# Three of seven local-attention value products on GpSimd, the activation's sign moved into w_in's columns

## The chip, the core and the metric

One core of a Trainium2 chip runs the whole program. The metric is device time in microseconds (us), the median of the runs of one program. The engines have an instruction queue each and run it strictly in order: PE (TensorE, matrix products; PEld is its weight load), DVE (VectorE), ACT (ScalarE), POOL (GpSimd) and SP, which here only issues the DMA transfers. An instruction whose input is not there yet holds up everything behind it on its engine. POOL works on on-chip SBUF only; the results of PE stand in PSUM, which DVE and ACT can read and write.

## The reference, cut to what matters

```python
B, H, S, D, factor = 8, 8, 576, 64, 4
# attention, per batch and head
q_d, k_d, v_d = means over 4 neighbouring tokens                # 144 tokens
out_up    = repeat(softmax(q_d @ k_d.T / 8) @ v_d, 4)
out_local = softmax(where(|i - j| < 4, q @ k.T / 8, -1e9)) @ v  # 7 neighbours of each token
x = (out_up + out_local) as 4608 tokens x 512
# feed-forward
h = x @ w_in                                                    # 512 -> 2048
g = maximum(h, 0) + alpha * minimum(h, 0)                       # alpha per column
out = g @ w_out                                                 # 2048 -> 512
```

The inputs of the feed-forward arrive as 64-bit floats and are decoded on the chip.

## The kernel before, in words

The work has three strands that share the engines.

**Weights** (`load_weights`, L159). w_in and w_out come in four parts n = 0 to 3 of 512 columns or rows. A piece of 128x512 lands as raw 64-bit words; `decode` (L150) turns it into `temp` with one ACT and four DVE instructions (L152 to L156). Then it is split into a high and a low half of reduced precision: ACT writes the high one (`wih`, L206, `woh`, L203), and the low one is the difference (`wil` on DVE, L210, or on POOL through `sub`, L97; `wol` on DVE, L204). For w_out each row is multiplied on the way by `sign`, which is +1 where alpha is at most 1 and -1 elsewhere. The raw pieces take turns in a few slots, and SP can issue the next only when a slot is free. Part 3 goes through other buffers, once the first batch's attention is done.

**Feed-forward.** Tokens go in 18 chunks of 256, columns in 8 pairs of 128, so there are 144 steps. `h_step` (L633) has 24 matmuls (L642) into `ph`, then the activation: ACT writes t = slope*h for each of the two columns (L651), DVE takes the maximum of sign*h and t for each of the two (L654, `sign` as a scalar of each partition), ACT writes the high half `gh` (L656), POOL the low half `gl` = t - gh (L97). `out_step` (L680) has 12 matmuls (L690) with gh and gl. The h step stands two steps ahead of its out step (AH = 2).

**Attention.** The first batch is done ahead on PE. From batch 1 on, `local` (L532) takes units of 192 tokens, u = 3 to 23, on DVE: a token's row lies on a partition as two heads x 6 tokens, its keys and values with three neighbours on either side. It does the score products and sums for two halves of three tokens (L551, L553), the softmax, and the value products: for each half the acc of neighbour 0 (L593), products of neighbours 1 to 3 and of 4 and 5 (L596), five additions to acc (L598). Neighbour 6 is multiplied on POOL (L580), one instruction for each half, and the last DVE addition joins it (`x`, L600). acc and the weights of the neighbours stand in the PSUM tile `lb`. PE transposes x (L607), and `xf`, `xh` and `xl` become the feed-forward's operands. Beside it `down` (L237) does the attention over the means: for each pair of heads SP loads six tiles (`ldq`, `ldk`, `ldv`, two each, L228) into three buffers, POOL adds neighbours in them (L231) and writes the sums (`s2q`, `s2k`, `s2v`, L232), which gives the buffer back; PE transposes the sums (L249) and so on. There is one s2q and one s2k, so the next is written when PE has transposed the last.

**What sets the order.** The code interleaves the generators of units, downs and steps; a scheduler then fixes each engine's list, with priorities (`high_priority`) for the activation. k and q of a unit have one buffer each, v has two, and a unit's loads are issued by SP in line with the ld loads. An ld tile that lands late holds up POOL, and with it every gl behind it.

Of the kernel before, what the change touches and what calls it, by code (L numbers as in the profile page):

```python
# [9 lines left out]
F32 = mybir.dt.float32  # L10
# [3 lines left out]
ALU = mybir.AluOpType  # L14
# [32 lines left out]
LDB = 3  # L47
SB = 2
# [21 lines left out]
def tile_attention_moe(ctx: ExitStack, tc: tile.TileContext, q, k, v, w_in, w_out, alpha, out):  # L70
# [22 lines left out]
    def f32(ap):  # L93
        return ap.bitcast(F32)
# [39 lines left out]

    def load_alpha():
        nc.sync.dma_start(slope, alpha.rearrange("(f p) -> p f", p=128))
        nc.vector.tensor_scalar(sign, slope, 1.0, 2.0, op0=ALU.is_le, op1=ALU.mult)
        nc.vector.tensor_scalar(sign, sign, -1.0, None, op0=ALU.add)
        nc.vector.tensor_tensor(slope, slope, sign, op=ALU.mult)
# [19 lines left out]
    def load_weights():  # L159
        temp, turn = one.tile([128, 4, 512], I32, tag="slot3", name="temp"), 0  # L160
        for n in range(4):
            if n in (1, 2):
                for i, x in enumerate("hl"):
                    wi[i][n] = one.tile([128, 4, 512], F32R, tag=f"spare{8 - 4 * n + i}", name=f"wi{x}{n}")
                    wo[i][n] = one.tile([128, 4, 512], F32R, tag=f"spare{10 - 4 * n + i}", name=f"wo{x}{n}")
            for which, w in enumerate((wi, wo)):
# [5 lines left out]
                for c0 in (0, 2):  # L172
# [17 lines left out]
                    for r, c, m in pieces:  # L190
# [341 lines left out]
    def local(late, u):  # L532
# [27 lines left out]
        if jj != 1:  # L560
# [13 lines left out]
        nc.vector.tensor_tensor(ex[:, :, 6], ex[:, :, 6], rs, op=ALU.mult)  # L574
        nc.vector.tensor_tensor(pw[:, :, 0:6], ex[:, :, 0:6],
                                rs.unsqueeze(2).to_broadcast([128, 2, 6, 6]), op=ALU.mult)
        pv6 = []
        for half in range(2):
            t = late.tile([128, 2, 3, 64], F32, tag="pp", name=f"pv6_{u}_{half}", bufs=2)
            nc.gpsimd.tensor_tensor(  # L580
                t, window4(vt, half, 6, 1)[:, 0],
                ex[:, half, 6].rearrange("p (h t) -> p h t", h=2).unsqueeze(3).to_broadcast([128, 2, 3, 64]),
                op=ALU.mult)
            pv6.append(t)
        yield
        x = late.tile([128, 6, 2, 64], F32, tag="x", name=f"x{u}", bufs=XB)
# [5 lines left out]
        for half in range(2):  # L592
            nc.vector.tensor_tensor(acc, window4(vt, half, 0, 1)[:, 0], prob(half, 0, 1)[:, 0], op=ALU.mult)  # L593
            for d0, nd in ((1, 3), (4, 2)):
                pr = late.tile([128, 3, 2, 3, 64], F32, tag="prod", bufs=PB, name=f"pv{u}_{half}{d0}")
                nc.vector.tensor_tensor(pr[:, :nd], window4(vt, half, d0, nd), prob(half, d0, nd), op=ALU.mult)  # L596
                for i in range(nd):
                    nc.vector.tensor_tensor(acc, acc, pr[:, i], op=ALU.add)  # L598
                yield
            nc.vector.tensor_tensor(x[:, 3 * half:3 * half + 3].rearrange("p t h d -> p h t d"),  # L600
                                    acc, pv6[half], op=ALU.add)
# [31 lines left out]
    def h_step(st):  # L633
# [14 lines left out]
        with tc.high_priority(offset=HP):  # L648
# [3 lines left out]
            for j in range(2):  # L652
                f = 2 * fp + j
                nc.vector.scalar_tensor_tensor(t[:, j], ph[:, j], sign[:, f:f + 1], t[:, j],  # L654
                                               op0=ALU.mult, op1=ALU.max)
# [185 lines left out]
```

## Time and profile before

| what | value |
|---|---|
| median of 3 runs | 1140.39 us (1134.49, 1140.88, 1140.39) |
| profiled execution | 1138.52 us |
| its span, first to last instruction | 1136.7 us |
| mean granted TensorE clock | 0.926 |

In the rows of the prediction, a group reads: line, engine, operation, result <- inputs (by the program's names), shape, xcount | busy us, mean ns of one | idle time of the engine just before, and what ended it. A row of waits reads: engine, line <- what was waited for: us in total, times, longest. A row of a stretch reads: from:to, length, then the busy time of each engine and, in brackets, the number of its instructions. A row of the chain of work that ended last reads: start us, length us, what.

### The profile page before, as it was taken

The numbers are of one execution on the slowest core, as the hardware profiler recorded it, in microseconds if no ns is written. First come the engines' busy times: TensorE is split into PE (matmuls) and PEld (weight loads), VectorE is DVE, ScalarE is ACT, GpSimd is POOL, SyncE is SP. The second block draws the span as 40 slices with busy tenths as digits, with TensorE's granted clock in tenths as the row PEclk, the third lists the DMA queues.
The fourth block names the chain that finished last, engine by engine and source line by source line (L and its number), as shares of the span: only waits on it lengthen the run. The fifth ranks groups of instructions, "written<-read, shape, count | busy, mean of one in ns | idle before, by whom it ended". The sixth has DMA issues, their size and how long they took to land.

```text
span 1136.7 us, 17891 instructions
## 1 busy us (share of the span) xinstructions
PE 1005.7 (88%) x6402; PEld 879.8 (77%) x6402; DVE 861.4 (76%) x1467; ACT 454.7 (40%) x1223; POOL 526.4 (46%) x633
## 2 busy tenths in 40 slices
PE   5857797898768999889999999989999989999995
PEld 5646675696657898777888888878888878899994
DVE  7999496597847889678878988779887778895110
ACT  5767344242323443333444334344343425333221
POOL 4787474333434644544555543555537244333221
PEclk9756889798968999899999999999999989999998
DMA  8944612222222222221223222323222212100000
GB/s 181 240 150 145 189 43 86 65 83 76 66 92 77 87 100 87 92 87 65 80 95 109 85 80 89 105 76 101 88 92 82 96 58 78 54 19 19 1 20 19
DMA packets 57503, 98.26 MB, mean 86 GB/s; under 512 B 19910, under 2 KB 25286, under 8 KB 57414
## 3 DMA queue, kind: packets, MB, share of 16 engines
q1 hardware_dynamic: 57414, 97.12, 27.1%
q8 instruction: 50, 0.82, 0.3%
q14 instruction: 39, 0.32, 0.1%
HBM read 87.67 MB, written 9.44 MB: 85 GB/s over the span
## 4 chain that ended last, share of the span: by engine, by line
PE 53%; DMA 20%; DVE 11%; POOL 6%; SPq 4%; issue 3%; ACT 2%; ACTq 0%; POOLq 0%; DVEq 0%
PE o L690 26%; PE h L642 22%; DMA ldk<-in_k 10%; DMA q<-in_q 4%; DMA ldq<-in_q 3%; POOL gl L97 2%; SPq L348 2%; DVE temp L155 1%; SPq L499 1%; POOL ldv L100 1%; DVE temp L153 1%; PE pv L266 1%; DVE temp L156 1%; PE xp L607 1%; DMA raw<-in_moe_w_out 1%
## 5 line engine op out<-in xcount | busy, mean ns | idle before, releaser
L97 POOL TENSOR_TENSOR gl<-t,gh 128x512 fp32r<-128x512 f32 x144 | 187.0, 1301 | 238.5 <-ACT gh L656 221.3
L654 DVE SCALAR_TENSOR_TENSOR t<-h,sign,t 128x256 f32<-128x256 f32 x288 | 125.6, 478 | 165.1 <-ACT t L651 159.3
L690 PE MATMUL o<-woh,gl 128*128 128x512 f32 x576 | 193.7, 414 | 45.1 <-POOL gl L97 45.0
L651 ACT ACTIVATE t<-h,slope 128x256 f32<-128x256 f32 x288 | 120.3, 469 | 244.4 <-PE h L642 159.4
L642 PE MATMUL h<-xh,wih 128*128 128x256 f32 x1152 | 201.1, 291 | 1.0 <-DVE t L654 0.7
L690 PE MATMUL o<-woh,gh 128*128 128x512 f32 x576 | 190.2, 407 | 10.3 <-ACT gh L656 10.3
L642 PE MATMUL h<-xh,wil 128*128 128x256 f32 x1152 | 194.3, 288 | 1.0 <-DVE wil L210 1.0
L690 PE MATMUL o<-wol,gh 128*128 128x512 f32 x576 | 191.2, 409 | 0.0
L642 PE MATMUL h<-xl,wih 128*128 128x256 f32 x1152 | 188.0, 285 | 0.0
L642 PEld LDWEIGHTS h<-xh,wih 128*128 128x128 f32 x1152 | 174.0, 196 | 14.4 <-DVE t L654 2.4
L690 PEld LDWEIGHTS o<-woh,gl 128*128 128x128 f32 x576 | 110.4, 195 | 75.8 <-POOL gl L97 51.7
L642 PEld LDWEIGHTS h<-xh,wil 128*128 128x128 f32 x1152 | 163.1, 194 | 1.9 <-DVE wil L210 1.2
L642 PEld LDWEIGHTS h<-xl,wih 128*128 128x128 f32 x1152 | 159.9, 192 | 0.3
L656 ACT CAST gh<-t 128x512 fp32r<-128x512 f32 x144 | 89.4, 621 | 148.5 <-PE o L690 78.6
L551 DVE TENSOR_TENSOR qk<-k,qp 128x768 f32<-128x768 f32 (+1 forms) x126 | 135.0, 1081 | 0.0
L553 DVE TENSOR_REDUCE ls<-qk 128x12 f32<-128x768 f32 (+1 forms) x126 | 133.5, 1080 | 0.2
L690 PEld LDWEIGHTS o<-wol,gh 128*128 128x128 f32 x576 | 111.1, 195 | 24.9 <-issue 0.2
L690 PEld LDWEIGHTS o<-woh,gh 128*128 128x128 f32 x576 | 102.3, 194 | 25.2 <-ACT gh L656 10.5
L598 DVE TENSOR_TENSOR lb<-lb,pv 128x384 f32<-128x384 f32 x210 | 117.9, 562 | 4.0
L100 POOL TENSOR_TENSOR ldk<-ldk 72x256 f32<-72x256 f32 x56 | 45.2, 808 | 153.7 <-DMA ldk<-in_k 143.3
L596 DVE TENSOR_TENSOR pv<-v,lb 128x1152 f32<-128x1152 f32 x84 | 96.8, 1152 | 2.5
L100 POOL TENSOR_TENSOR ldq<-ldq 72x256 f32<-72x256 f32 x56 | 42.8, 774 | 80.6 <-DMA ldq<-in_q 80.4
(146 smaller groups left out, 1194.3 us busy)
## 6 DMA issues: line engine op xcount, KB each, us to landing
k<-in_k SPq DMA_DIRECT2D x41, 384.0 KB
v<-in_v SPq DMA_DIRECT2D x41, 384.0 KB
raw<-in_moe_w_in SPq DMA_DIRECT2D x16, 512.0 KB
raw<-in_moe_w_out SPq DMA_DIRECT2D x16, 512.0 KB
ldq<-in_q SPq DMA_DIRECT2D x56, 144.0 KB
ldk<-in_k SPq DMA_DIRECT2D x56, 144.0 KB
ldv<-in_v SPq DMA_DIRECT2D x56, 144.0 KB
q<-in_q SPq DMA_DIRECT2D x42, 192.0 KB
```

Source lines behind the costliest of these rows:

```text
L97: nc.gpsimd.tensor_tensor(o, a, b, op=ALU.subtract)
L100: nc.gpsimd.tensor_tensor(o, a, b, op=ALU.add)
L348: nc.sync.dma_start(qk[hp][:, i, :, e, :], bass.AP(src.tensor, (2 * hp + e) * HEAD, [[512, 72], [64, 8], [1, 64]]))
L551: nc.vector.tensor_tensor(pr[:, :nd], window(kt, half, d0, nd), qp.unsqueeze(1).to_broadcast([128, nd, 2, 192]), op=ALU.mult)
L553: nc.vector.tensor_reduce(out=s[:, half, d0:d0 + nd, :].rearrange("p a b -> p (a b)"), in_=pr[:, :nd].rearrange("p a h (t d) -> p (a h t) ...
L596: nc.vector.tensor_tensor(pr[:, :nd], window4(vt, half, d0, nd), prob(half, d0, nd), op=ALU.mult)
L598: nc.vector.tensor_tensor(acc, acc, pr[:, i], op=ALU.add)
L642: nc.tensor.matmul(ph[:, j], w[:, m, 128 * o:128 * o + 128], x[:, m, :], start=(i == 0), stop=(i == 11))
L651: nc.scalar.activation(t[:, j], ph[:, j], AF.Copy, scale=slope[:, f:f + 1])
L654: nc.vector.scalar_tensor_tensor(t[:, j], ph[:, j], sign[:, f:f + 1], t[:, j], op0=ALU.mult, op1=ALU.max)
L656: nc.scalar.copy(gh, t)
L690: nc.tensor.matmul(po, g[:, j, 128 * m:128 * m + 128], wo[w][n][:, o, :], start=(f == 0 and i == 0), stop=(f == NF - 1 and i == 2))
```

## The change

1. Of the seven neighbours, 4, 5 and 6 (`FAR` = 3) now go to POOL: for each half three products and two additions there, the first product straight into x's tile. DVE keeps neighbours 0 to 3 (one product of one, one of three, three additions) and adds acc to what POOL left in x. v is read by POOL three times as often, and its buffer is free when both engines are done.
2. The sign leaves the activation: w_in's columns are multiplied by it (a DVE instruction for each of w_in's 16 pieces of 128x512, before the halves are taken), from a row of signs that is made once for each n from a DMA of alpha to all partitions and two DVE instructions. The rows of w_out keep theirs. ACT's slope is now alpha itself.
3. The two maxima of a step become one, of 128x512, of ph and t.

```diff
+FAR = 3
+    def to_sign(o, a):
+        nc.vector.tensor_scalar(o, a, 1.0, 2.0, op0=ALU.is_le, op1=ALU.mult)
+        nc.vector.tensor_scalar(o, o, -1.0, None, op0=ALU.add)
...
-        nc.vector.tensor_tensor(slope, slope, sign, op=ALU.mult)
+        to_sign(sign, slope)
+    def column_signs(n):
+        row = two.tile([128, DM], F32, tag="stage", name=f"srow{n}", bufs=SB)
+        nc.sync.dma_start(row, bass.AP(alpha.tensor, 512 * n, [[0, 128], [1, 512]]))
+        to_sign(row, row)
+        return row
...
+            srow = column_signs(n)
...
                             else:
+                                nc.vector.tensor_tensor(f32(t), f32(t), srow.unsqueeze(1).to_broadcast([128, m, 512]), op=ALU.mult)
                                 nc.scalar.copy(wh, f32(t))
...
+        ND = 7 - FAR
+        x = late.tile([128, 6, 2, 64], F32, tag="x", name=f"x{u}", bufs=XB)
+        xs = [x[:, 3 * half:3 * half + 3].rearrange("p t h d -> p h t d") for half in range(2)]
         for half in range(2):
-            t = late.tile([128, 2, 3, 64], F32, tag="pp", name=f"pv6_{u}_{half}", bufs=2)
-            nc.gpsimd.tensor_tensor(
-                t, window4(vt, half, 6, 1)[:, 0],
...
+            for i, dl in enumerate(range(ND, 7)):
+                o = xs[half] if i == 0 else late.tile([128, 2, 3, 64], F32, tag="pp", name=f"pv{dl}_{u}_{half}", bufs=2)
+                nc.gpsimd.tensor_tensor(
+                    o, window4(vt, half, dl, 1)[:, 0],
...
+                if i:
+                    add(xs[half], xs[half], o)
+            yield
...
         for half in range(2):
             nc.vector.tensor_tensor(acc, window4(vt, half, 0, 1)[:, 0], prob(half, 0, 1)[:, 0], op=ALU.mult)
-            for d0, nd in ((1, 3), (4, 2)):
-                pr = late.tile([128, 3, 2, 3, 64], F32, tag="prod", bufs=PB, name=f"pv{u}_{half}{d0}")
-                nc.vector.tensor_tensor(pr[:, :nd], window4(vt, half, d0, nd), prob(half, d0, nd), op=ALU.mult)
-                for i in range(nd):
-                    nc.vector.tensor_tensor(acc, acc, pr[:, i], op=ALU.add)
-                yield
-            nc.vector.tensor_tensor(x[:, 3 * half:3 * half + 3].rearrange("p t h d -> p h t d"),
-                                    acc, pv6[half], op=ALU.add)
+            pr = late.tile([128, 3, 2, 3, 64], F32, tag="prod", bufs=PB, name=f"pv{u}_{half}")
+            nc.vector.tensor_tensor(pr, window4(vt, half, 1, 3), prob(half, 1, 3), op=ALU.mult)
+            for i in range(3):
+                nc.vector.tensor_tensor(acc, acc, pr[:, i], op=ALU.add)
+            yield
+            nc.vector.tensor_tensor(xs[half], acc, xs[half], op=ALU.add)
...
-            for j in range(2):
-                f = 2 * fp + j
-                nc.vector.scalar_tensor_tensor(t[:, j], ph[:, j], sign[:, f:f + 1], t[:, j],
-                                               op0=ALU.mult, op1=ALU.max)
+            nc.vector.tensor_tensor(t, ph, t, op=ALU.max)
```

The scheduler also gives every engine another order. Three places follow; before's lines are those of the kernel before, the others those of the changed kernel (L595 and L101 are the products and additions on POOL, L614 is the last addition on DVE, L665 the maximum, L203 the raw loads, L239 the ld loads).

POOL around unit 8, before: the products of neighbour 6 and what stands behind them up to the next two gl.

```order
L97 TENSOR_TENSOR gl_4201<-t_4199,gh_4200 128x512
L580 TENSOR_TENSOR pv_8_0_3826<-v_3170,lex_3767 128x384
L580 TENSOR_TENSOR pv_8_1_3828<-v_3170,lex_3767 128x384
L100 TENSOR_TENSOR ldv_20_4083<-ldv_20_4083 72x2x128
L100 TENSOR_TENSOR ldv_21_4087<-ldv_21_4087 72x2x128
L100 TENSOR_TENSOR ldq_30_4263<-ldq_30_4263 72x2x128
L100 TENSOR_TENSOR s2v_2_4082<-ldv_20_4083 72x2x64
L100 TENSOR_TENSOR s2v_2_4082<-ldv_21_4087 72x2x64
L97 TENSOR_TENSOR gl_4298<-t_4296,gh_4297 128x512
```

POOL at the same place now, from the first product of unit 8 to the first addition of its second half.

```order
L595 TENSOR_TENSOR pv_8_0_3794<-v_3185,lex_3731 128x384
L595 TENSOR_TENSOR x_3789<-v_3185,lex_3731 128x2x3x64
L98 TENSOR_TENSOR gl_4155<-t_4153,gh_4154 128x512
L101 TENSOR_TENSOR ldq_30_4272<-ldq_30_4272 72x2x128
L101 TENSOR_TENSOR x_3789<-x_3789,pv_8_0_3791 128x2x3x64
L98 TENSOR_TENSOR gl_4239<-t_4237,gh_4238 128x512
L101 TENSOR_TENSOR ldq_31_4276<-ldq_31_4276 72x2x128
L101 TENSOR_TENSOR ldk_30_4288<-ldk_30_4288 72x2x128
L101 TENSOR_TENSOR x_3789<-x_3789,pv_8_0_3794 128x2x3x64
L595 TENSOR_TENSOR pv_8_1_3807<-v_3185,lex_3731 128x384
L98 TENSOR_TENSOR gl_4343<-t_4341,gh_4342 128x512
L101 TENSOR_TENSOR x_3789<-x_3789,pv_8_1_3807 128x2x3x64
```

Ten instructions of the unit are spread over the ld adds and the gl, where two stood in a row; ld adds that wait for a transfer now stand between a half's products and its last addition.

DVE in unit 8, before: from the end of the first half to the second half's first products (t is the maximum of a step).

```order
L654 SCALAR_TENSOR_TENSOR t_4296<-h_4271,sign,t_4296 128x256 x2
L598 TENSOR_TENSOR lb_3766<-lb_3766,pv_01_3841 128x384
L596 TENSOR_TENSOR pv_04_3846<-v_3170,lb_3766 128x768
L598 TENSOR_TENSOR lb_3766<-lb_3766,pv_04_3846 128x384 x2
L600 TENSOR_TENSOR x_3839<-lb_3766,pv_8_0_3826 128x2x3x64
L593 TENSOR_TENSOR lb_3766<-v_3170,lb_3766 128x384
```

DVE at the same place now.

```order
L612 TENSOR_TENSOR lb_3730<-lb_3730,pv_0_3814 128x384 x2
L665 TENSOR_TENSOR t_4237<-h_4212,t_4237 128x512
L665 TENSOR_TENSOR t_4341<-h_4316,t_4341 128x512
L614 TENSOR_TENSOR x_3789<-lb_3730,x_3789 128x2x3x64
L608 TENSOR_TENSOR lb_3730<-v_3185,lb_3730 128x384
```

The addition that joins POOL's part now stands two maxima later, and the second half, which uses the same acc, stands behind it.

SP near the end of the start, before: the pieces of w_in's part 3 (raw_1036, raw_1055) among the loads.

```order
L228 DMA ldk_20_1402<-in_k 72x512
L193 DMA raw_1036<-in_moe_w_in 128x1024 x2
L228 DMA ldk_21_1406<-in_k 72x512
L193 DMA raw_1055<-in_moe_w_in 128x1024 x2
L228 DMA ldv_20_1411<-in_v 72x512
```

SP now (raw_1063 and raw_1084 are those pieces).

```order
L239 DMA ldq_31_1560<-in_q 72x512
L239 DMA ldk_30_1565<-in_k 72x512
L203 DMA raw_1063<-in_moe_w_in 128x1024 x2
L239 DMA ldk_31_1569<-in_k 72x512
L239 DMA ldv_30_1574<-in_v 72x512
L203 DMA raw_1084<-in_moe_w_in 128x1024 x2
```

The last part of w_in is loaded one down later than before; in exchange the ld loads of the downs behind it stand ahead of the next v and q.

More of the change, by code (lines that the diff above doesn't have):

```diff
@@ L573, in local @@
         acc = lb[:, 0:384].rearrange("p (h t d) -> p h t d", h=2, t=3)
[L574 to L577, printed above, removed]
-        for half in range(2):
-            t = late.tile([128, 2, 3, 64], F32, tag="pp", name=f"pv6_{u}_{half}", bufs=2)
-            nc.gpsimd.tensor_tensor(
-                t, window4(vt, half, 6, 1)[:, 0],
-                ex[:, half, 6].rearrange("p (h t) -> p h t", h=2).unsqueeze(3).to_broadcast([128, 2, 3, 64]),
-                op=ALU.mult)
-            pv6.append(t)
-        yield
-        x = late.tile([128, 6, 2, 64], F32, tag="x", name=f"x{u}", bufs=XB)
+        ND = 7 - FAR
+        nc.vector.tensor_tensor(ex[:, :, ND:], ex[:, :, ND:], rs.unsqueeze(2).to_broadcast([128, 2, FAR, 6]), op=ALU.mult)
+        nc.vector.tensor_tensor(pw[:, :, 0:ND], ex[:, :, 0:ND],
+                                rs.unsqueeze(2).to_broadcast([128, 2, ND, 6]), op=ALU.mult)
+        x = late.tile([128, 6, 2, 64], F32, tag="x", name=f"x{u}", bufs=XB)
+        xs = [x[:, 3 * half:3 * half + 3].rearrange("p t h d -> p h t d") for half in range(2)]
+        for half in range(2):
+            for i, dl in enumerate(range(ND, 7)):
+                o = xs[half] if i == 0 else late.tile([128, 2, 3, 64], F32, tag="pp", name=f"pv{dl}_{u}_{half}", bufs=2)
+                nc.gpsimd.tensor_tensor(
+                    o, window4(vt, half, dl, 1)[:, 0],
+                    ex[:, half, dl].rearrange("p (h t) -> p h t", h=2).unsqueeze(3).to_broadcast([128, 2, 3, 64]),
+                    op=ALU.mult)
+                if i:
+                    add(xs[half], xs[half], o)
+            yield
         def prob(half, d0, nd):
```

3 lines of the change are left out of this document (removed).

## The prediction

> **What bounds the kernel now.** I read first how busy each engine is over the whole span, then the chain of work that ended last, then stretches of time, and last the waits of the stretch that turned out to matter. The page's own lines:
>
> ```profile
> span 1136.7 us, 17891 instructions
> PE 1005.7 (88%) x6402; PEld 879.8 (77%) x6402; DVE 861.4 (76%) x1467; ACT 454.7 (40%) x1223; POOL 526.4 (46%) x633
> ...
> PE 53%; DMA 20%; DVE 11%; POOL 6%; SPq 4%; issue 3%; ACT 2%; ACTq 0%; POOLq 0%; DVEq 0%
> ```
>
> PE is the bound on average, but of the chain it holds only 53%, and transfers hold 20%: there are places where PE waits. The stretches tell them apart. A row gives from:to, length, busy time of PE, PEld, DVE, ACT and POOL with instruction counts, then the granted clock, the DMA share and GB/s.
>
> ```profile
> 0.00:50.00 50.00, 34.02 (x212) 29.73 (x213) 41.31 (x79) 30.48 (x79) 26.20 (x43) 0.90 0.93 199
> 50.00:100.00 50.00, 32.31 (x222) 25.82 (x221) 48.85 (x81) 32.91 (x95) 40.09 (x34) 0.53 0.51 160
> 213.00:960.00 747.00, 689.51 (x4433) 605.42 (x4434) 611.90 (x1038) 290.89 (x808) 354.11 (x457) 0.96 0.25 84
> 360.00:460.00 100.00, 99.97 (x671) 89.27 (x670) 92.29 (x158) 43.81 (x119) 45.61 (x56) 1.00 0.27 93
> 960.00:1137.00 177.00, 164.50 (x1050) 147.35 (x1048) 82.75 (x153) 52.74 (x117) 45.36 (x39) 0.98 0.07 24
> ```
>
> The start (0 to 213) decodes weights; 213 to 960 is the steady part, where units, downs and steps run together; behind it only steps are left. From 0 to 50 the DMA engines are the full ones (0.93), from 50 to 100 DVE is (48.85 of 50). How far the steady part is from its own best pace is seen by counting the two feed-forward lines in it and in its best 100 us. First the h matmuls (L642), then the out matmuls (L690); the columns are PE and PEld of that line alone:
>
> ```profile
> 213.00:960.00 747.00, 337.39 (x2508) 322.03 (x2508) 0.96 0.25 84
> 360.00:460.00 100.00, 50.96 (x388) 48.66 (x388) 1.00 0.27 93
> ```
>
> ```profile
> 213.00:960.00 747.00, 336.75 (x1256) 233.86 (x1256) 0.96 0.25 84
> 360.00:460.00 100.00, 49.34 (x193) 34.66 (x192) 1.00 0.27 93
> ```
>
> A step has 24 + 12 = 36 of them. The steady part does (2508 + 1256) / 36 = 104.6 steps at 7.14 us, the best stretch (388 + 193) / 36 = 16.1 steps at 6.20. So the steady part loses 104.6 x 0.94 = 98 us against a pace that this kernel itself reaches, with PE at 99.97 and DVE at 92.29 of 100. DVE's load does not set the pace there, then; something stops PE now and then. The waits of that stretch (what waits <- for what: us, times, longest):
>
> ```profile
> POOL ldk L100 <- DMA ldk<-in_k: 128.7, 23, 16.9
> POOL gl L97 <- ACT gh L656: 107.5, 31, 9.2
> POOL ldq L100 <- DMA ldq<-in_q: 59.7, 23, 10.2
> PE o L690 <- POOL gl L97: 45.0, 16, 5.7
> DVE x L600 <- POOL pv L580: 13.5, 6, 6.0
> SPq L520 <- DVE pv L596: 92.0, 12, 23.2
> ```
>
> PE's largest wait is for gl on POOL, 45.0 us; POOL in turn stands 128.7 + 59.7 = 188.4 us before ld tiles that have not landed. The chain shows one such ring (start, length, what):
>
> ```profile
> 284.68 0.14 PE qkT L249 x2
> ...
> 284.88 0.47 POOL s2q L100
> 285.37 10.38 DMA ldk<-in_k
> ```
>
> PE's transposes free s2q, POOL writes the next sums, that frees an ld buffer, SP loads into it for 10.38 us, and POOL waits at the next ld add, with gl behind it and PE behind gl. Of every us that POOL waits for ld transfers, 45.0 / 188.4 = 0.24 reaches PE; I use 0.24 as the price of a late POOL or SP.
>
> **The change part by part.** The instructions concerned, as groups (busy us, mean ns of one | idle before it):
>
> ```profile
> L654 DVE SCALAR_TENSOR_TENSOR t<-h,sign,t 128x256 f32<-128x256 f32 x288 | 125.6, 478 | 165.1 <-ACT t L651 159.3 <-POOL gl L97 1.7 <-POOL s2v L100 1.4
> L598 DVE TENSOR_TENSOR lb<-lb,pv 128x384 f32<-128x384 f32 x210 | 117.9, 562 | 4.0
> L596 DVE TENSOR_TENSOR pv<-v,lb 128x768 f32<-128x768 f32 x42 | 40.0, 952 | 1.2
> L580 POOL TENSOR_TENSOR pv<-v,lex 128x384 f32<-128x384 f32 x42 | 34.0, 828 | 3.8 <-PE o L690 3.3 <-issue 0.3
> ```
>
> *DVE is relieved.* Per half the product of neighbours 4 and 5 and two additions go: 42 x (0.952 + 2 x 0.562) = 87.2 us. 288 maxima of 256 become 144 of 512. None of that size is in the trace; the DVE rows of 384 (0.562) and 768 (0.952) bound one, and a third of the way between them is 0.692, so 99.6 us stand for 125.6, 26 less (between 45 less and 11 more). Together 113 us, of which some 100 fall in the steady part. All of it would count if DVE set the pace, but the best stretch says that it doesn't. What a freer DVE does is to give buffers back earlier: SP waits 12 times for DVE's products, 92.0 us, with ld loads queued behind. Each product chain of a unit is 4.2 us shorter (2 x 2.08), so those waits shrink by at most 12 x 4.2 = 50 us; times 0.24 that is 12 us. I take **-12**, with 0 (the ring of the transposes has no DVE in it) and -49 (half of the 98) as ends.
>
> *POOL is loaded, and tied to DVE.* 84 products more at 0.828 are 69.6 us. 84 additions of 384 lie between these rows of the steady part, which also show the load adds:
>
> ```profile
> L97 POOL TENSOR_TENSOR gl<-t,gh 128x512 fp32r<-128x512 f32 x106 | 136.0, 1286 | 120.1 <-ACT gh L656 107.5 <-PE o L690 7.1 <-PE h L642 4.3
> ...
> L100 POOL TENSOR_TENSOR ldk<-ldk 72x256 f32<-72x256 f32 x45 | 33.0, 734 | 138.5 <-DMA ldk<-in_k 128.7 <-DVE pv L596 9.8
> L100 POOL TENSOR_TENSOR ldq<-ldq 72x256 f32<-72x256 f32 x44 | 31.7, 731 | 60.0 <-DMA ldq<-in_q 59.7 <-PE pT L293 0.3
> ```
>
> Halfway between 734 and 1286 is 1.01 us, so 84.7 us: 154 us in all, 7.3 per unit. In the steady part POOL now has 354.1 busy and 188.4 waiting for ld tiles, 542.5 of 747 (73%); with 19 units of 7.3 it has 681 (91%) if the waits stay. So POOL does not become the bound, but its slack goes from 27% to 9%. The Trainium skill (GPSIMD Engine Reference, section Performance versus the Vector engine) says that an elementwise operation of two inputs takes GpSimd about twice DVE's time. The rows here give 828 against 562 for 384 elements, 1.47 times. By the page the moved work would be an estimated 168 x 2 x 0.562 = 189 us instead of 154, and the sum some 8 us higher; the row is of this very shape, and I stay with it.
>
> The larger part is the order. Before, two POOL products stand in a row early in the unit, and DVE waited for them only 13.5 us. Now ten POOL instructions stand spread, and in 18 of 21 units adds of ldq or ldk stand between the first product and the last addition, 47 of them in all. About half of such adds wait (23 of 45 and 23 of 44), 188.4 / 46 = 4.1 us each: 23.5 x 4.1 = 96 us that DVE's final addition of a half can now wait for. What is queued behind that on DVE is the second half (same acc), and the maxima of the following steps, hence gh, gl and PE's out step. At 0.24 that is **+23**. Lower end 0: DVE's spare 100 us absorb it. Upper end 48, half of it. By another reading, the moved instructions that stand between an ld add and the next gl (47 against 14) delay gl by 0.7 us net at each of 16 stalls, +11; both fall on the same waits, so only the larger counts. v is now given back by the slower of two engines; that too is a part of this term.
>
> *The start.* 16 column products of 128x512 and 8 instructions that make the sign rows are new on DVE. Rows of the start (groups, then single instructions with the wait before them in brackets):
>
> ```profile
> L156 DVE SCALAR_TENSOR_TENSOR temp<-raw,temp 128x512 int32<-128x512 int32 x32 | 27.5, 864 | 0.1
> L153 DVE TENSOR_SCALAR temp<-temp 128x512 f32<-128x512 f32 x32 | 22.6, 709 | 11.3 <-ACT temp L152 11.3
> ...
> L210 DVE TENSOR_TENSOR wil<-temp,wih 128x512 fp32r<-128x512 f32 x11 | 10.9, 995 | 0.0
> ```
>
> ```profile
> 135.49 1.96 DVE L153 TENSOR_SCALAR temp<-temp 128x512 f32<-128x512 f32 x1 [8.13 <-ACT temp L152]
> ...
> 142.68 3.02 DVE L156 SCALAR_TENSOR_TENSOR temp<-raw,temp 128x512 int32<-128x512 int32 x1
> ```
>
> 16 x 0.995 + 8 x 0.709 = 21.6 us, 5.4 for each of four parts. The first lies in 0 to 50, where DVE is idle 8.7 us behind the transfers: nothing. The second and third fall in 50 to 100, where DVE is full: 10.8 on the path. The fourth comes behind 135, with the loads of part 3. The DVE wait of 8.13 at 135.49 takes up half of these 16.2; I take **+8**. Upper end 32: the products stretch to 3.02 each, as that one row did beside POOL work, (3.02 - 0.995) x 16. Lower end -14, from SP's order: the ld loads stand ahead of v and q now, and POOL's longest wait for one between 181 and 213 could go. Against it, w_in's part 3 is issued one down later. That wait:
>
> ```profile
> POOL ldk L100 <- DMA ldk<-in_k: 13.9, 1, 13.9
> ```
>
> The sign rows' four DMAs are 256 KB each on the chip's side, beside 512 KB pieces from 0 to 50; hidden there.
>
> *The rest.* The slopes and signs per column are tiny. ACT and PE keep their counts. Behind 960 DVE has 82.75 of 177, and the merged maximum is hidden by that idle time.
>
> Sum: 8 - 12 + 23 = +19 on the profiled execution's 1138.52 (span and 1.8 around it): 1157.5. That execution is 1.9 under the median of 1140.39, so **1159**.
>
> **The rivals.** *The relief reaches PE (faster).* If the rings close faster because SP's loads for DVE-held buffers no longer delay the ld loads, and POOL's additions fit into its waits, half of the 98 us comes back and the coupling costs nothing: 1138.5 + 8 - 49 + 1.9 = 1099. For it speak the 92.0 us of SP's waits for DVE products and the 125.6 us of maxima on the path from ph to gl, which DVE does sooner; against it the ring above, in which DVE has no part. It decides where DVE's final additions wait for POOL under some 40 us in all.
>
> *It cancels (same).* If the ld adds between the moved instructions are seldom late, only the +11 counts: 1138.5 + 8 - 12 + 11 + 1.9 = 1147. For it speaks that half of the adds didn't wait before.
>
> *DVE and POOL block each other (slower still).* The row at 142.68 took 3.02 us where 32 of its kind took 0.864 on average, and POOL was at work there. If each column product waits so, the start costs +32 more than the work, and 8 + 32 - 12 + 23 gives 1138.5 + 51 + 1.9 = 1191. The Trainium skill (SBUF — State Buffer, section Who interferes with whom) has such a rule: a DVE instruction with two SBUF inputs and a GpSimd instruction that reads SBUF exclude each other, the second waits for the whole of the first. Against it stands the mean of L210, 995 ns, with two SBUF inputs and POOL busy up to 40.09 of 50: most are not held up for long.
>
> *The change doesn't do what it says:* DVE's relief is eaten by waits for POOL. That is the mechanism of my forecast.
>
> **How the numbers follow.** Against the median, 1% is 1129.0 and 1151.8, about what a measurement of this kernel can tell from no change. The forecast has 0.48 and its own range of 1152 to 1182 (the coupling from +16 to +46); blocking 0.06, beyond 1182; cancelling 0.16; the relief 0.30. So slower 0.54, same 0.16, faster 0.30. The range has to hold both signs: its low end is the relief's own 1098, below which half of that case's 0.30 lies, its high end 1195, just past the blocking rival's 1191, with 0.05 beyond. That leaves out 0.2.
>
> **What would show it.** In the changed profile, from 213 to 960: DVE's wait for POOL at the last addition grows from 13.5 to some 100 us; POOL's busy share rises from 47% to about 66%; PE's wait for gl rises from 45.0 towards 70; DVE's busy time falls by some 100. In the start, 50 to 100 stays full on DVE, the first steady out step comes some 8 us later, and the column products take about 1.0 us (0.7 to 1.0). The forecast is wrong if DVE's wait for POOL stays under 40 us, or if the steady part takes less than 7.0 us per step: then the relief counted. It is wrong upward if the column products take 2 us or more, or if POOL's additions take far more than 1.01.

## The result, and the profile after

| | before | changed |
|---|---|---|
| median, us | 1140.64 (4 runs, 1134.49 to 1145.43) | 1193.27 (4 runs, 1191.89 to 1194.83) |
| ratio, 95% interval | | 1.0478 (1.0422 to 1.0534) |
| mean granted TensorE clock, profiled run | 0.926 | 0.906 |

The change costs 53 us. The time lies within the range and on the side of the forecast, but the forecast of 1159 was 19 us above before: the loss was mis-sized nearly threefold. First the page's own lines of the changed kernel:

```profile
span 1191.0 us, 17740 instructions
...
PE 1020.0 (86%) x6402; PEld 890.4 (75%) x6402; DVE 766.8 (64%) x1220; ACT 457.3 (38%) x1223; POOL 661.3 (56%) x801
...
PE 30%; DMA 28%; POOL 16%; DVE 12%; issue 6%; SPq 4%; ACT 2%; ACTq 0%; POOLq 0%; DVEq 0%
```

DVE lost 95 us of work and POOL gained 135 (its new products and additions take 155, other work there took some 20 less). PE does the same 6402 matmuls, but holds only 30% of the chain where it held 53%; transfers and POOL hold 28% and 16%. PE's 54 us are two things: it is idle for 1191.0 - 1020.0 = 171 us where it was idle for 131, and the matmuls themselves take 14 us longer, at a granted clock of 0.906 for 0.926.

The stretches, columns as in the prediction, and the h and out matmuls (L655, L700) of the steady part:

```profile
50.00:100.00 50.00, 30.68 (x240) 23.00 (x239) 50.00 (x83) 31.69 (x94) 36.16 (x38) 0.64 0.52 161
...
213.00:960.00 747.00, 648.53 (x4045) 566.17 (x4044) 483.22 (x769) 269.35 (x748) 449.62 (x569) 0.92 0.24 80
```

```profile
213.00:960.00 747.00, 312.13 (x2274) 296.36 (x2275) 0.92 0.24 80
```

```profile
213.00:960.00 747.00, 314.35 (x1138) 219.29 (x1136) 0.92 0.24 80
```

(2274 + 1138) / 36 = 94.8 steps in 747 us, 7.88 us a step where before had 7.14. Neither DVE (483 of 747) nor POOL (450) is near full. Where the time goes shows in the start of the gh of each step, read from the timeline of ACT (us):

| step | before | changed | difference |
|---|---|---|---|
| 9th | 179.7 | 187.4 | +7.7 |
| 17th | 252.8 | 238.7 | -14.1 |
| 25th | 334.1 | 317.4 | -16.6 |
| 65th | 606.0 | 634.0 | +27.9 |
| 121st | 988.0 | 1045.5 | +57.6 |
| last | 1118.5 | 1173.1 | +54.6 |

All of the loss, 74 us, falls between the 25th and the 121st step, where units run. The start, in contrast, was some 17 us shorter. The waits of the same stretch, 213 to 960:

```profile
POOL ldk L101 <- DMA ldk<-in_k: 168.6, 23, 14.3
DVE x L614 <- POOL x L101: 73.1, 17, 9.9
PE o L700 <- POOL gl L98: 60.7, 17, 8.5
DVE xf L628 <- POOL xl L98: 35.3, 5, 11.6
POOL ldq L101 <- DMA ldq<-in_q: 34.8, 11, 7.7
...
PE xp L620 <- DVE x L614: 18.0, 7, 6.7
```

DVE's last addition of a half waits 73.1 us for POOL (13.5 before), PE waits 60.7 for gl (45.0). DVE also waits 35.3 at xf, which is one tile: the next part can be written only when POOL has made xl from the last. PE now waits 18.0 us directly for DVE's last addition, at the transposes of x (0.2 before), a way that the forecast did not name. POOL's own waits for ld transfers hardly grew: over the whole span 228.1 us before and 237.0 now, ldq, ldk and ldv together. What grew is what stands behind them. One such moment, first from the chain and then from DVE's timeline:

```profile
577.51 0.64 POOL gl L98
578.15 14.56 DMA ldk<-in_k
...
592.84 0.41 POOL ldk L101
...
595.33 0.79 POOL x L595
596.12 0.93 POOL pv L595 x2
...
598.48 1.22 POOL gl L98
```

```profile
600.67 0.69 DVE L665 TENSOR_TENSOR t<-h,t 128x512 f32<-128x512 f32 x1 [14.58 <-ACT t L664]
605.79 0.56 DVE L614 TENSOR_TENSOR x<-lb,x 128x384 f32<-128x384 f32 x1 [4.42 <-POOL x L101]
```

A late ldk stops POOL from 578 to 593. The unit's products stand behind it, then gl, then the additions; DVE stands still 14.6 us before a maximum and 4.4 us more before its last addition.

### The profile page after: what moved, and what is told of

Read it like the earlier page. It is cut to its first block, busy times and chain, and to the rows that moved or that the text cites. A ratio compares the mean times of both kernels' runs of the same rounds, so it can differ in the third digit from the quotient of the medians.

```text
span 1191.0 us, 17740 instructions
## 1 busy us (share of the span) xinstructions
PE 1020.0 (86%) x6402; PEld 890.4 (75%) x6402; DVE 766.8 (64%) x1220; ACT 457.3 (38%) x1223; POOL 661.3 (56%) x801
## 4 chain that ended last, share of the span: by engine, by line
PE 30%; DMA 28%; POOL 16%; DVE 12%; issue 6%; SPq 4%; ACT 2%; ACTq 0%; POOLq 0%; DVEq 0%
DMA ldk<-in_k 19%; PE o L700 15%; PE h L655 13%; DMA q<-in_q 3%; POOL gl L98 3%; DMA ldv<-in_v 3%; POOL x L101 2%; POOL ldv L101 2%; DMA ldq<-in_q 2%; DVE qk L562 2%; POOL pv L595 2%; SPq L359 2%; DVE temp L165 1%; POOL s2k L101 1%; DVE ls L564 1%
## 5 line engine op out<-in xcount | busy, mean ns | idle before, releaser
L700 PE MATMUL o<-woh,gl 128*128 128x512 f32 x576 | 198.7, 422 | 61.9 <-POOL gl L98 61.9
L665 DVE TENSOR_TENSOR t<-h,t 128x512 f32<-128x512 f32 x144 | 98.8, 686 | 204.0 <-ACT t L664 192.6
L655 PE MATMUL h<-xh,wih 128*128 128x256 f32 x1152 | 204.3, 295 | 11.9 <-DVE t L665 6.0
L655 PEld LDWEIGHTS h<-xh,wih 128*128 128x128 f32 x1152 | 176.2, 198 | 25.5 <-DVE t L665 7.0
L655 PE MATMUL h<-xh,wil 128*128 128x256 f32 x1152 | 194.8, 290 | 0.0
L700 PE MATMUL o<-woh,gh 128*128 128x512 f32 x576 | 191.8, 410 | 3.2 <-ACT gh L666 3.2
L655 PE MATMUL h<-xl,wih 128*128 128x256 f32 x1152 | 192.7, 287 | 0.0
L700 PE MATMUL o<-wol,gh 128*128 128x512 f32 x576 | 190.7, 410 | 0.6 <-DVE wol L214 0.6
L700 PEld LDWEIGHTS o<-woh,gl 128*128 128x128 f32 x576 | 112.6, 200 | 93.7 <-POOL gl L98 69.1
L655 PEld LDWEIGHTS h<-xh,wil 128*128 128x128 f32 x1152 | 164.8, 197 | 0.9 <-issue 0.4
L655 PEld LDWEIGHTS h<-xl,wih 128*128 128x128 f32 x1152 | 162.8, 195 | 0.2 <-issue 0.2
L101 POOL TENSOR_TENSOR ldk<-ldk 72x256 f32<-72x256 f32 x56 | 42.7, 762 | 181.1 <-DMA ldk<-in_k 181.1
L700 PEld LDWEIGHTS o<-wol,gh 128*128 128x128 f32 x576 | 112.0, 196 | 26.9 <-DVE wol L214 1.0
L700 PEld LDWEIGHTS o<-woh,gh 128*128 128x128 f32 x576 | 103.8, 196 | 18.9 <-ACT gh L666 3.8
L628 DVE TENSOR_TENSOR xf<-xp,od 128x128 f32<-128x128 f32 (+1 forms) x105 | 40.8, 437 | 78.7 <-POOL xl L98 49.3
L101 POOL TENSOR_TENSOR x<-x,pv 128x384 f32<-128x384 f32 x84 | 85.0, 1012 | 0.7
L614 DVE TENSOR_TENSOR x<-lb,x 128x384 f32<-128x384 f32 x42 | 23.2, 551 | 79.1 <-POOL x L101 79.0
```

The lines of the kernel that those rows point to most:

```text
L101: nc.gpsimd.tensor_tensor(o, a, b, op=ALU.add)
L628: nc.vector.tensor_tensor(xf.rearrange("p a t (s e) -> p e t a s", e=2)[:, par, j0:j0 + nj], tp.rearrange("p (t a s e) -> p e t a s", t=4, ...
L655: nc.tensor.matmul(ph[:, j], w[:, m, 128 * o:128 * o + 128], x[:, m, :], start=(i == 0), stop=(i == 11))
L665: nc.vector.tensor_tensor(t, ph, t, op=ALU.max)
L700: nc.tensor.matmul(po, g[:, j, 128 * m:128 * m + 128], wo[w][n][:, o, :], start=(f == 0 and i == 0), stop=(f == NF - 1 and i == 2))
```

## The experiments

My theory was the forecast's (A): DVE's last addition waits for POOL. Its rivals: POOL's work makes gl and the ld sums late without that wait (B), and the new activation and column products cost more than they save (C).

All ratios are to runs of the kernel before on the same chip (95% interval). Every variant also gets its own order from the scheduler, so differences under some 10 us between two of them are not given a cause.

**1. Which part costs.** Part 1 alone, and parts 2 and 3 alone.

```diff
far_only:  the changed kernel with
...
-                                nc.vector.tensor_tensor(f32(t), f32(t), srow.unsqueeze(1)..., op=ALU.mult)
...
-            nc.vector.tensor_tensor(t, ph, t, op=ALU.max)
+            for j in range(2): nc.vector.scalar_tensor_tensor(t[:, j], ph[:, j], sign..., t[:, j], ...)
sign_only: the kernel before with the opposite edits
```

> Part 1 alone: three neighbours on POOL, but the activation's sign and the two maxima as before. Between its first and last unit the changed kernel lost some 74 us against before, and its start was some 15 us shorter. Theory A (DVE's last addition of a half waits for POOL, with everything behind it in DVE's order) and theory B (POOL's 154 us more of work make gl and the ld adds late by themselves) both put the loss into part 1: 1190 to 1215, the upper end if the shorter start belongs to parts 2 and 3. Theory C (the loss comes from the single maximum, which waits for both of ACT's writes, and from the column products): at most 1155.

Measured 1184.5, ratio 1.0423 (1.0391 to 1.0455), somewhat under what A and B put.

> Parts 2 and 3 alone: sign in w_in's columns, one maximum for two steps, neighbours as before. A and B: 1115 to 1145, the lower end if the start's 15 us come from here. C: 1175 or more.

Measured 1128.4, ratio 0.9938 (0.9916 to 0.9960). Parts 2 and 3 cost nothing by themselves (7 us faster, less than the 10 above); theory C falls. Part 1 carries the loss.

**2. The wait, or the work?**

```diff
uncoupled:
-                o = xs[half] if i == 0 else late.tile([128, 2, 3, 64], F32, tag="pp", ...)
+            o = [late.tile([128, 2, 3, 64], F32, tag="pp", ...) for i in range(2)]
...
-                    add(xs[half], xs[half], o)
+                    add(o[0], o[0], o[1])
-            nc.vector.tensor_tensor(xs[half], acc, xs[half], op=ALU.add)
+            nc.vector.tensor_tensor(xs[half], acc, pr[:, 0], op=ALU.add)
no_far: the same last addition, and no POOL products or additions
```

> The changed kernel, but POOL's products and additions of neighbours 4 to 6 go to a tile of their own which nobody reads; DVE's last addition of the same size takes another operand. The result lacks these neighbours. POOL's and DVE's work stay as in the changed kernel, only DVE's wait for POOL is gone. A: the loss goes with the wait, 1110 to 1140. B: the loss stays, 1175 or more. Something between would share it out.

Measured 1173.5, ratio 1.0317 (1.0276 to 1.0359): most of the loss stays.

> As the kernel without the wait, and POOL doesn't make the products and additions of neighbours 4 to 6 at all (the result lacks them). This is DVE's relief with neither the wait nor the load. A: within 12 us of the kernel without the wait, 1100 to 1135. B: 50 us or more below it, 1090 to 1125.

Measured 1115.3, ratio 0.9815 (0.9779 to 0.9852). The wait that my forecast rested on is worth some 18 us (4.78 - 3.17 = 1.61% of 1136, give or take 8). POOL's work with no reader is worth 57. Theory A is too small by itself; B has the larger share.

**3. What of the work?** POOL's time, its place, or what it holds.

```diff
free:   ident * slope (constants) in place of v * ex, in the kernel "uncoupled"
place:  ident * ex, and ex with bufs=2
unc_lex2: v * ex, and ex with bufs=2
hold:   place, and behind the unit's last POOL addition
+            if half == 1:
+                nc.gpsimd.tensor_tensor(o[0][:, 0, 0, 0:1], vt[:, 0, 0, 0:1], o[0][:, 0, 0, 1:2], op=ALU.mult)
```

> The kernel without the wait (1174) lost 58 us against the one without POOL's value work (1115). Here POOL does the same count, sizes and operations as in the kernel without the wait, but on constant tiles, so that it waits for no unit and neither v's nor the softmax weights' buffer is held by it (the result lacks neighbours 4 to 6). Theory B1 (POOL's time itself: gl, xl and the ld sums stand behind it): 1160 or more. Theory B2 (POOL gives v and the weights back late, which delays the next unit's loads and its softmax): at most 1135.

Measured 1140.4, ratio 1.0067 (1.0045 to 1.0089): B1 as put there falls, and B2's bound is missed by 5 us. Two stretches of the kernel without POOL's work (no_far) and of this one, in this order:

```profile
100.00:213.00 113.00, 95.67 (x553) 81.76 (x553) 100.40 (x144) 54.97 (x142) 60.40 (x61) 0.86 0.38 125
213.00:960.00 747.00, 697.89 (x4533) 614.01 (x4532) 546.93 (x881) 300.12 (x832) 327.72 (x424) 0.97 0.26 87
```

```profile
100.00:213.00 113.00, 81.66 (x444) 68.69 (x444) 104.68 (x118) 50.12 (x129) 92.22 (x91) 0.77 0.33 109
213.00:960.00 747.00, 688.47 (x4462) 604.71 (x4462) 548.45 (x867) 296.01 (x825) 475.35 (x596) 0.97 0.26 89
```

Part of POOL's work ran early, from 100 to 213 (92 of 113 us busy), and there PE made 109 matmuls fewer. In the steady part POOL is busy for 475 us, more than in the changed kernel, and PE makes 4462 matmuls for 4533: 1.6% fewer, 12 us, with 172 of the 210 added instructions there. POOL's time by itself is cheap there.

> As the kernel without the wait (1174), but POOL multiplies the unit's softmax weights with a constant tile and not with v (the result lacks neighbours 4 to 6), and the weights have two buffers, so POOL's work stands at the unit's time and holds up neither v's buffer nor the next softmax. The kernel with the same load on constants alone gave 1140, of which some 18 us were lost ahead of the first unit, where its work could run early. Theory P (POOL's work at the unit's time, in the way of gl, xl and the ld sums): 1160 or more. Theory V (v's buffer is given back late, SP stands at the next v load with the ld loads behind it): 1115 to 1135.

Measured 1139.3, ratio 1.0023 (1.0001 to 1.0046), between the two expectations and nearer V's.

> The kernel without the wait (1174), with two buffers for the unit's softmax weights; POOL multiplies v by them again. Against the run on constants in v's place (1139) only v's reading is added, against the kernel without the wait only the weights' second buffer. Theory V (v given back late): 1160 to 1180. Theory L (the weights given back late, so that the next softmax waits): 1130 to 1145.

Measured 1180.1, ratio 1.0390 (1.0356 to 1.0425): the weights' buffer is not it. So three kernels in which POOL reads v last take 1174, 1180 and (below) 1185 us, and the two in which it doesn't 1140 and 1139, though each has an order of its own.

> The run on constants in v's place (1139), with one more POOL instruction for each unit behind its last addition, which reads one element a partition of v. POOL's work is the same but for 21 tiny instructions; v's buffer is held until it, as with the real products. Theory V (it is the hold of v's buffer): 1165 to 1185, and SP's wait for POOL before v loads back at some 50 us. If it is the reading of v itself (access beside DVE, 210 reads): 1135 to 1145.

Measured 1185.1, ratio 1.0411 (1.0368 to 1.0453). SP's waits before loads of k and v (L531) in place, in unc_lex2 and in hold:

```profile
SPq L531 <- DVE pv L610: 92.2, 9, 20.3
```

```profile
SPq L531 <- POOL pv L595: 49.4, 12, 10.1
SPq L531 <- DVE pv L610: 46.9, 4, 16.4
```

```profile
SPq L531 <- POOL pv L602: 59.3, 14, 11.5
SPq L531 <- DVE pv L612: 41.0, 4, 13.5
```

21 reads of one element a partition bring back 3.88% (44 us). So it is the release of v's buffer and not the reading. In place no wait for POOL stands in these rows; in hold there are 14, 59.3 us. DVE's are shorter in exchange, so SP stands before v loads for hardly longer, 100 us for 92. What differs is when the load is issued: in the mean of 19 loads 2.4 us after DVE's last read of the buffer in place, 13.9 in hold, 10.8 in unc_lex2 (from the timelines of SP and DVE).

How this reaches PE is not shown. POOL's waits for ld transfers did not grow (208.3 us in place, 203.8 in hold, whole span), nor did PE's wait for gl (40.5 and 34.2). DVE's wait for k did, which is loaded behind v; place first, then hold:

```profile
DVE qk L562 <- DMA k<-in_k: 10.3, 3, 5.7
```

```profile
DVE qk L562 <- DMA k<-in_k: 36.1, 5, 13.9
```

It is 10.3 in no_far and free too, and 29.6 and 27.7 in uncoupled and unc_lex2. In hold PE is idle for 30 us more than in place, and that much more before the matmuls of the downs (L260, L271, L277 and L304: 31.7 us in place, 64.0 in hold); in unc_lex2, idle for 23 us more, it is not there (32.7).

**4. Less of it, and more room.**

```diff
far2:   FAR = 2, DVE's products in two groups of two
gl_dve: -            sub(gl, t, f32(gh))
        +            nc.vector.tensor_tensor(gl, t, f32(gh), op=ALU.subtract)
ldb4:   LDB = 4 (for 3), "pp" bufs=1
v3:     "vt" bufs=3 (for 2), PB = 1 (for 2), "pp" bufs=1
far3_vlate: load_kv(late, u + 1, "v") moved behind load_kv(late, u + 1, "k")
```

> Two neighbours on POOL for three: 78 us more POOL work than with one, against 120 in the changed kernel. From 1128 (one, with parts 2 and 3) to 1193 (three), a loss in proportion to POOL's work gives 1128 + 65 x 78 / 120 = 1170 (1160 to 1180). A loss that sets in only when POOL has no slack left gives 1125 to 1150.

Measured 1150.8, ratio 1.0161 (1.0140 to 1.0181). By the ratios the second neighbour costs 25 us over sign_only and the third 36 more. POOL's busy time shows about the same added work for each (516.4, 592.9 and 661.3 us with one, two and three), not the 78 and 42 us that I had expected. So the cost grows somewhat faster than the work, and it sets in while POOL still has slack (52% busy with two). DVE's wait for POOL at the last addition is already 74.9 us with two neighbours, over the whole span, and 79.0 with three: its length alone doesn't set the loss.

> The changed kernel whole, with gl (144 subtractions, 186 us on POOL) made on DVE instead. POOL's busy time falls below that of the kernel before, DVE's returns to about it. B1: what stood behind POOL's work is freed, 1100 to 1145. B2: the value work still gives its buffers back as soon as POOL's queue lets it, which is sooner too, 1130 to 1165. If DVE's load or its waits for POOL are what counts, since the maxima and gl now stand behind them: 1165 or more.

Measured 1205.0, ratio 1.0632 (1.0603 to 1.0661), against both B theories; it meets the third reading, 1165 or more. POOL's busy time is 502.3 and DVE waits still longer for it; gl itself is quick on DVE. First the waits, then the group:

```profile
POOL ldk L101 <- DMA ldk<-in_k: 150.2, 33, 17.5
DVE x L614 <- POOL x L101: 136.3, 18, 12.6
```

```profile
L667 DVE TENSOR_TENSOR gl<-t,gh 128x512 fp32r<-128x512 f32 x144 | 119.9, 832 | 43.2 <-ACT gh L666 42.8
```

POOL, 42% busy, still stands 150 us before ldk, and 180.6 us before xl for ACT's xh; what makes it late is what it waits for rather than its work. With gl on DVE more of the activation stands behind DVE's wait for POOL. That fits the coupling of the forecast at a higher price, but no run takes that wait out of this kernel.

> The changed kernel with four ld buffers for three (the products' scratch on POOL, which only POOL uses, has one buffer for two, to make room). If POOL's lateness reaches PE through the ring of the ld buffers (late sums, late loads, POOL waits at the add, gl behind it): 1140 to 1175. If it reaches PE directly, gl behind value work: 1185 to 1200.

Measured 1194.2, ratio 1.0547 (1.0513 to 1.0580): one more ld buffer gains nothing here. POOL's waits for ld transfers did fall, from 237.0 us to 167.0, while DVE's wait for POOL rose from 79.0 to 101.5.

> The changed kernel whole, with three v buffers for two; the room comes from the scratch of products, which only one engine uses, one buffer for two on DVE and on POOL. SP's load of v can no longer wait for POOL's or DVE's last read of the unit before. V: 1150 to 1175. P: 1180 to 1200.

Measured 1189.6, ratio 1.0443 (1.0389 to 1.0497). DVE's wait for POOL grows, and SP's waits before v loads do not go away. DVE's first, then SP's in the changed kernel and in this one, all of the whole span:

```profile
DVE x L614 <- POOL x L101: 150.2, 30, 16.1
```

```profile
SPq L531 <- DVE pv L610: 87.9, 14, 20.1
...
SPq L531 <- POOL pv L595: 16.9, 13, 6.3
```

```profile
SPq L531 <- DVE pv L610: 135.0, 14, 19.8
...
SPq L531 <- POOL pv L595: 24.8, 16, 4.1
```

The scheduler used the third buffer to put each v load a unit earlier in SP's order, so SP still stands there until the last read of a unit: of unit 3 for the load of unit 6, where it was unit 5. The premise of the expectation, that SP can no longer wait there, didn't hold, and the run decides nothing about v's hold.

> The changed kernel whole, with SP's load of the next unit's v issued behind that of its k in the middle of a unit and no longer at its start, when the last unit's v may still be read. If the late release of v's buffer reaches PE through SP's queue (v load waits, ld loads behind it): 1150 to 1175. If DVE's wait for POOL takes the loss over, as with three v buffers (1190): 1180 to 1200.

Measured 1188.9, ratio 1.0500 (1.0461 to 1.0539). SP's row of waits for DVE at these loads, 87.7 us in 14, stands as in the changed kernel (87.9 in 14), so the move hardly took the wait away and says little. No run, then, removes v's hold alone from the whole changed kernel. There the load is issued 1.1 us after DVE's last read in the mean: DVE, which waits for POOL, reads v as late as POOL does.

**5. The ring loosened.**

```diff
before_ld, sign_ld, far3_ld:
-PB = 2
+PB = 1
-LDB = 3
+LDB = 4
-..., tag=f"s2{x}", ..., bufs=S2B if x == "v" else 1)
+..., tag=f"s2{x}", ..., bufs=S2B)
```

> Parts 2 and 3 alone (1128), with DVE's scratch of products single, and the room given to a fourth ld buffer and to second tiles for the sums s2q and s2k. The ring of transposes, sums and ld loads that I read from the profile before was put at 98 us of stalls; if it is made of too few buffers, 1085 to 1115. If it is SP's order or transfers late for another reason: 1120 to 1135.

Measured 1089.2, ratio 0.9573 (0.9542 to 0.9604): the fastest kernel of the study, 4.3% below before. Its page, and two waits of its whole span:

```profile
PE 984.7 (91%) x6402; PEld 867.5 (80%) x6402; DVE 873.7 (80%) x1346; ACT 456.4 (42%) x1223; POOL 530.5 (49%) x633
...
PE 65%; DVE 13%; DMA 10%; POOL 4%; issue 2%; ACT 2%; SPq 2%; ACTq 0%; POOLq 0%; DVEq 0%
```

```profile
POOL ldk L100 <- DMA ldk<-in_k: 86.8, 26, 7.7
...
PE o L697 <- POOL gl L97: 12.9, 7, 5.0
```

PE's wait for gl is 12.9 us (45.0 before, 23.6 in sign_only), and transfers fall from 20% of the chain to 10%. POOL's waits for ld transfers fall little in sum (203.0 us, 218.4 in sign_only); the longest is 9.3 us where it was 13.4. Which of the added buffers does it was not tried. DVE is busier (80%) than in any slow variant: its load was not the limit.

> The kernel before with that looser ring and nothing else. If the ring is worth the same with and without parts 2 and 3: 1095 to 1105. If DVE's shorter maxima are worth more once the ring is loose: 1105 to 1120.

Measured 1105.6, ratio 0.9747 (0.9703 to 0.9790): 29 us for the ring alone. Parts 2 and 3 then bring 20 more (0.9747 - 0.9573), for 7 with the tight ring.

> The changed kernel whole, with the looser ring that took parts 2 and 3 from 1128 to 1089: a fourth ld buffer, second tiles for s2q and s2k, DVE's scratch of products single. If POOL's late sums in that ring carry the loss, it shrinks from 65 us to under 30: 1095 to 1120. If the loss is DVE's wait, POOL's work ahead of gl and v's buffer, none of which this loosens: 1145 to 1175.

Measured 1140.7, ratio 1.0041 (1.0018 to 1.0063). By the ratios part 1 costs 53 us with the loose ring (1.0041 - 0.9573 of 1136), 61 with the tight one (1.0478 - 0.9938). Neither expectation is met; most of part 1's loss is not in the number of these buffers.

> The same with the looser ring (1141 without the later v load). If v's release is what is left there: 1105 to 1125. If DVE's wait and POOL's work at the unit's time are: 1132 to 1150.

Measured 1142.0, ratio 1.0074 (1.0045 to 1.0104), no change.

> Parts 2 and 3 with the looser ring (1089) and the later v load, for the fastest version. SP waited 74 us for DVE's products before v loads there: 1075 to 1090 if some of it reaches PE, 1087 to 1100 if the load then comes late instead.

Measured 1089.5, ratio 0.9614 (0.9586 to 0.9643), no change either. In both, SP's waits for DVE before v loads stayed (128.8 us for 128.3 in far3_ld, 72.6 for 74.0 in sign_ld), so these runs say as little about v's release as far3_vlate.

## Why the prediction was right or wrong

Taking the parts away one after the other, from the changed kernel down, the ratios give (1% is 11.4 us). Each row is uncertain by 3 to 8 us, and each pair also differs in the scheduler's order:

| step | runs | us |
|---|---|---|
| parts 2 and 3 | sign_only to before | -7 |
| DVE's relief by part 1, POOL's old product gone | no_far to sign_only | -14 |
| POOL's work at the unit's time | place to no_far | +24 |
| v held until POOL has read it, DVE's wait already gone | uncoupled to place | +33 |
| DVE's wait for POOL at the last addition | changed to uncoupled | +18 |
| sum | | +54 |

*The place of the loss: right.* It lies in the steady part, where transfers stop POOL and others stand behind POOL. Loosening the ring alone gave 29 us of the 98 that I counted there, with parts 2 and 3 49.

*The signs that I named* came, most of them smaller: DVE's wait 73.1 us (100 said), POOL 60% busy in the steady part (66%), PE's wait for gl 60.7 (70). The loss was larger all the same.

*DVE's relief, -12: right in size* (-14), as far as no_far shows it, which also lacks POOL's old products. SP's waits for DVE before v loads fell from 101.8 us (sign_only) to 63.8, the way that I gave. That 95 us off DVE are worth so little fits the reading that its load doesn't set the pace.

*The coupling, +23: near for what it named* (+18), in part by luck. 18 is what it gives to remove DVE's wait while v's hold stays and takes over (SP's loads then come 10.7 us after DVE's last read, 1.1 in the changed kernel), and PE also met this wait at the transposes of x, which I hadn't named.

*The step that failed* is the price of part 1: -12 + 23 = +11 in the forecast, 61 measured (1.0478 - 0.9938). It failed in the sentence that the two readings "fall on the same waits, so only the larger counts", by which POOL's own work was dropped, and in the one behind it, that v's later release "is a part of this term". With DVE's wait gone (uncoupled), 57 of the 75 us that part 1 costs over its relief are still there. 24 of them are POOL's work without v, where I had +11. 33 come with v's hold (42 and 44 by the pairs unc_lex2 and hold to place), and I gave it no price. For it I should have read the row of SP's 92.0 us of waits before v loads both ways: as something that DVE's relief shortens, and as a load that a late reader on POOL puts off.

How the shares divide depends on the order of removal. In the whole changed kernel POOL's lateness shows as DVE's wait, and v comes back hardly later by POOL than by DVE; what v's hold alone would give back there is not shown. Where both ties are cut, some 52 us of the loss go (changed to place). So the two are one lateness with two ways on, and how the second of them reaches PE is open.

*POOL's load: right in size, not the cause by itself.* The additions took 1.012 us (1.01 said), the products 0.832. free has 172 of its 210 added instructions in the steady part, for 12 us there; at the unit's time (place) 184 of them cost 30 us there (4350 matmuls for 4533). The 91% that I worked out for POOL adds waits for transfers to its work; free shows that work which doesn't depend on a unit finds room in them.

*The start, +8: half right.* At the 9th step the changed kernel is 7.7 us late and far_only, without column products, 1.7 early (sign_only, with them, 6.1 late), so the products do cost about what was said. By the 17th step it is 14.1 us ahead, the lower end that I gave, and by the 25th 16.6: that gain hid as much of the loss behind it. The cause is not the one that the column products could have, since far_only is 13.2 ahead there and sign_only 13.6; SP's order, which I named, is different in all of them, but it wasn't tried alone.

*The rivals.* The relief falls with DVE's wait of 73.1 us (under 40 was its condition), cancelling with part 1's 61. Blocking is seen, but at a small price. The group of the column products, then the same instructions by shortest, median and longest (ns):

```profile
L216 DVE TENSOR_TENSOR temp<-temp,srow 128x512 f32<-128x512 f32 x16 | 14.8, 924 | 0.0
```

```profile
L216 DVE TENSOR_TENSOR temp<-temp,srow x16: 673/678/2731, 19.6 to 166.5; 128x512 f32<-128x512 f32 x16
```

Eleven of the 16 took 673 to 679 ns. The other five took 0.94 to 2.73 us, and each of them had POOL instructions beside it, the longest four in a row; of the eleven only four had any. Against 678 the five are 4 us longer in all, where the rival had 32. The rule of the Trainium skill (SBUF — State Buffer, section Who interferes with whom) agrees with these five, though no run here set the two engines side by side on purpose. The merged maximum took 0.686 us (0.692 said).

*The range.* It held the time only by its upper end of 1195, which was set just past the blocking rival's 1191; the forecast's own part ended at 1182. As blocking was not what cost the time, that was luck.

## What to carry to other kernels

Before work is moved to an idle engine, list what it reads, who waits for those buffers, and what the engine itself waits for: an in-order engine that stops for transfers hands its lateness to every buffer that it now reads last (44 us here for 21 tiny reads) and to every result that someone joins in order. In this kernel idle time that is made of such stops took work that nobody waits for at a low price (12 us in the steady part), and work tied to a unit at a high one. Where a profile shows stalls that a ring of small buffers makes, room for the ring (here 4 KB a partition, taken from a scratch that a single engine uses) can be worth more than the relief of a busy engine (29 us against 14 here). And a run that is meant to remove a wait proves something only if its trace shows the wait gone: the third v buffer left it in place.

## What the hardware showed besides

The same 6402 matmuls were busy for 984.7 us in the fastest kernel, 1005.7 before and 1020.0 after, at mean granted clocks of 0.937, 0.926 and 0.906: in these three PE ran its matmuls slower where it waited more, some 14 of the 54 us here. It is no rule. The profiled execution of before_ld, at 1099 us, had a clock of 0.969 and 988.4 us of matmuls, and the runs of the kernel before that went beside the experiments had clocks from 0.917 to 0.954 while their times stayed within 1128 to 1142 us. What sets the clock was not tried.
